# Wider weight rows, and another order of the output rows, in a decode block on one NeuronCore

## The chip, the cores and the metric

The kernel runs on one core of a Trainium2 chip. The metric is the device time of one launch in microseconds. The kernel before takes 121.06 us, the median of six runs (121.66, 121.75, 120.92, 120.96, 121.12 and 121.01 us).

## What is computed

A decode step for 8 sequences of one token each (B = 8, D = 512): a layer norm, and on its result two branches. Branch A is attention with 32 query heads over 8 key/value heads, on the last 1024 positions of a 4096-long cache (W = Sk // 4). Branch B is a gated feed-forward net with F = 1792. They meet in the last line.

```
xn = _layernorm(x)
q  = xn @ wq                                  # [512, 4096], 32 heads of 128
p  = softmax(q @ k[last 1024].T * 128**-0.5)  # 8 kv heads, 4 queries to each
s  = (p @ v[last 1024]) @ wo                  # [4096, 512]
g  = silu((gelu(xn @ w_gate) * (xn @ w_up)) @ w_down)
out = x + s * g                               # [8, 512]
```

All inputs are bf16. Keys and values of the window are 16 MB each, wq and wo 4 MB each, the three feed-forward weights 1.75 MB each (MB of 2^20 bytes here; the profile's page counts in 10^6).

## The kernel before

**Tiles and loads.** The attention is cut into 16 groups g = (b, i): one sequence b, and the half i of the kv heads (HN = 4 heads); the loop runs over i outside and b inside. A group needs one K tile and one V tile of 1 MB each: [128 partitions, 4096] bf16, so a partition holds 8 KB. All loads of weights, keys and values go into one ring of NSLOT = 20 such slots (`slot()`), and SyncE (SP) issues them in program order: wq in four pieces of 128 rows (L85, 8 KB to a partition) with the first K tile behind the first piece; then the second K tile, and in the loop V of group g and K of group g + 2 (L90). In the last group follow w_gate, w_up and w_down in two halves each (L100, L110: 7 KB to a partition), and in the round after it wo (L120, L125). The seven pieces of wo hold 8, 8, 8, 4, 2, 1 and 1 of its 32 steps, a step being one contraction of 128 rows; a partition takes four consecutive rows of wo per head group, so what lies together is 4 KB (2 and 1 KB in the last pieces). Between the third and the fourth piece four small loads put x into `x_res` (L499).

The framework gives the DMAs eight completion semaphores in turn, so each DMA of SP also waits until the eighth DMA before it has landed.

**A group.** TensorE transposes K (`turn_k`, L247, into PSUM; copied out by VectorE and ScalarE, L253), multiplies with the query (`score`, L263 and L273), ScalarE takes the exponential (L286), VectorE transposes it (L294), TensorE multiplies with V (`values`, L307), and `gather` (L323, L327, L336, L337) sums, divides and writes the head outputs into `oT_all`, laid out [d, half, kv head, query, b]. In round g the scores of group g stand before the values and the gather of group g - 1.

**Before the groups.** xhat (L210), [8, 512] padded to 32 rows, is transposed twice: in 128-column blocks for wq (L220), and with a stride of four for the feed-forward weights, whose partition p holds rows 4p to 4p + 3 (L223). The query projection is 32 matmuls (L375), eight for each piece of wq.

**The end.** After each half of the groups `regroup(i)` brings `oT_all` into the order of the rows of wo: 16 matmuls with columns of the identity (L350) and one copy into `og` (L359). Then `ffn_up` has 16 matmuls with w_gate and 16 with w_up (L418), the gelu (L430 to L442) and a VectorE transpose (L445); `ffn_down` has 28 matmuls (L461) and the silu (L473 to L480). The output projection is 64 matmuls (L537): for each of the 32 steps of wo, one for each half of the 512 columns. The two of a step sit on different columns of the array and run side by side; they are called a pair below. Two VectorE operations (L548, L549) and two small stores end the kernel. The schedule is written out by hand[...].

Of the kernel before, what the change touches and what calls it, by code (L numbers as in the profile page):

```python
# [11 lines left out]
BF16 = mybir.dt.bfloat16  # L12
FP32 = mybir.dt.float32
# [3 lines left out]
def kernel(  # L17
# [13 lines left out]
    nc = tc.nc  # L31

    B, Sq, D = A_x.shape
    Hkv, Sk, Dh = A_k_cache.shape[1], A_k_cache.shape[2], A_k_cache.shape[3]
    Hq = A_wq.shape[1] // Dh
    rep = Hq // Hkv
# [10 lines left out]

    NHALF = 2
    HN = Hkv // NHALF
    NSLOT = 20  # L50
    SLOT = NSC * Dh * HN
    NKR = W * HN // P
    QW = HN * rep
# [1 line left out]
    FR = F // P  # L55

    consts = ctx.enter_context(tc.tile_pool(name="consts", bufs=1))
    ring = ctx.enter_context(tc.tile_pool(name="ring", bufs=NSLOT))
    persist = ctx.enter_context(tc.tile_pool(name="persist", bufs=1))
    kT_pool = ctx.enter_context(tc.tile_pool(name="kT_pool", bufs=2))  # L60
# [13 lines left out]
    def slot():  # L74
        return ring.tile([P, SLOT], BF16, name="slot", align_bytes=512)

    x_flat = A_x.flatten_outer_dims()
    x_sb = persist.tile([B, D], BF16, name="x_sb")
    x_res = persist.tile([P, D // 2], BF16, name="x_res")
    nc.gpsimd.memset(x_res, 0.0)  # L80


    def load_wq(k):
        t = slot()
        nc.sync.dma_start(out=t, in_=A_wq[k * P : (k + 1) * P, :])  # L85
        return t

    def load_kv(cache, b, i):
        t = slot()
# [5 lines left out]
        )  # L95
        return t

    def load_up(w, k2):
        t = slot()
        nc.sync.dma_start(  # L100
            out=t[:, 0 : 2 * F],
            in_=w.rearrange("(p k) n -> p (k n)", k=NDC)[:, 2 * k2 * F : 2 * (k2 + 1) * F],
        )
        return t

    def load_down(h):
        t = slot()
        n = FR // 2 * D
        rows = B_w_down.rearrange("(p j) d -> p (j d)", j=FR)
        nc.sync.dma_start(out=t[:, 0:n], in_=rows[:, h * n : (h + 1) * n])  # L110
        return t

    wo_rows = A_wo.rearrange("(hh p j) d -> p hh (j d)", p=P, j=rep)

    def load_wo(h0, j0, j1):

        t = slot()
        n = (j1 - j0) // rep if j1 - j0 > rep else 1
        if n > 1:
            nc.sync.dma_start(  # L120
                out=t[:, 0 : n * rep * D].rearrange("p (h f) -> p h f", h=n),
                in_=wo_rows[:, h0 : h0 + n, :],
            )
        else:
            nc.sync.dma_start(  # L125
                out=t[:, 0 : (j1 - j0) * D],
                in_=wo_rows[:, h0, j0 * D : j1 * D],
            )
        return t

    groups = [(b, i) for i in range(NHALF) for b in range(B)]
# [1 line left out]
    k_t, v_t = {}, {}  # L133
    wq_t = [load_wq(0)]
    k_t[0] = load_kv(A_k_cache, *groups[0])
    wq_t += [load_wq(k) for k in range(1, NDC)]
    k_t[1] = load_kv(A_k_cache, *groups[1])


# [14 lines left out]
        base=0,  # L154
        pattern=[[-1, P]],
        channel_multiplier=1,
    )
    ident_f = consts.tile([P, P], FP32, name="ident_f")
    nc.vector.tensor_copy(out=ident_f, in_=ident)
# [55 lines left out]
        op0=ALU.subtract,  # L215
        op1=ALU.mult,
    )
    xT_ps = ps_t.tile([P, 2, NDC, 32], BF16, name="t_ps", tag="t")
    for k in range(NDC):
        nc.tensor.transpose(  # L220
            xT_ps[:, 0, k, :], xhat[:, k * P : (k + 1) * P], ident[0:32, 0:32]
        )
        nc.tensor.transpose(  # L223
            xT_ps[:, 1, k, :],
            xhat.rearrange("b (p k) -> b k p", k=NDC)[:, k, :],
            ident[0:32, 0:32],
        )
    xT = persist.tile([P, 2, NDC, 32], BF16, name="xT")
    nc.vector.tensor_copy(out=xT, in_=xT_ps)

    q2_all = persist.tile([P, NHALF, B, 2, 2, HN, rep], BF16, name="q2_all")
    nc.gpsimd.memset(q2_all, 0.0)
    oT_all = persist.tile([P, NHALF, HN, rep, B], BF16, name="oT_all")
    og = persist.tile([P, Hkv * rep + 1, 32], BF16, name="og")
    nc.vector.memset(og, 0.0)

    kT_t, p_t, pT_t, ss_t, o_t = {}, {}, {}, {}, {}
# [80 lines left out]
    def gather(g):  # L320
        b, i = groups[g]
        a_ps = ps_a.tile([P, 2, QW], FP32, name="a_ps", tag="a")
        nc.tensor.matmul(  # L323
            a_ps[:, 0, :], ones_f, ss_t[g], start=True, stop=True, skip_group_check=True
        )
        for r in range(2):
            nc.tensor.matmul(  # L327
                a_ps[:, 1, :],
                o_t[g][:, r * Dh : (r + 1) * Dh],
                selr[:, r, :],  # L330
                start=(r == 0),
                stop=(r == 1),
                skip_group_check=True,
            )
        rs = small.tile([P, QW], FP32, name="rs")
        nc.vector.reciprocal(out=rs, in_=a_ps[:, 0, :])  # L336
        nc.vector.tensor_tensor(  # L337
            out=oT_all[:, i, :, :, b],
            in0=a_ps[:, 1, :].rearrange("p (n j) -> p n j", n=HN),
            in1=rs.rearrange("p (n j) -> p n j", n=HN),  # L340
            op=ALU.mult,
        )

    def regroup(i):

        rg = ps_a.tile([P, rep, HN, B], FP32, name="rg_ps", tag="a")
        sel = ident.rearrange("p (e j) -> p j e", j=rep)
        for j in range(rep):
            for c in range(rep):
                nc.tensor.matmul(  # L350
                    rg[32 * c : 32 * c + 32, j, :, :],
                    sel[:, j, :],
                    oT_all[:, i, :, c, :],
                    start=True,
                    stop=True,
                    skip_group_check=True,
                    tile_position=(0, 32 * c),
                )
        nc.vector.tensor_copy(  # L359
            out=og[:, i * HN * rep : (i + 1) * HN * rep, 0:B].rearrange(  # L360
                "p (h j) b -> p h j b", j=rep
            ),
            in_=rg.rearrange("p j h b -> p h j b"),
        )


# [4 lines left out]
    for k in range(NDC):  # L371
        for i in range(NHALF):
            for j in range(HN):
                n0 = (HN * i + j) * 512
                nc.tensor.matmul(  # L375
                    q_ps[i][32 * j : 32 * j + 32, :],
                    xT[:, 0, k, :],
                    wq_t[k][:, n0 : n0 + 512],
                    start=(k == 0),
                    stop=(k == NDC - 1),  # L380
                    tile_position=(0, 32 * j),
                    skip_group_check=True,
                )
# [28 lines left out]
    def ffn_up():  # L412
        z_ps = ps_big.tile([P, 512], FP32, name="big")
        u_ps = ps_big.tile([P, 512], FP32, name="big")
        for ps, ws in ((z_ps, wg_t), (u_ps, wu_t)):
            for k in range(NDC):
                for j in range(4):
                    nc.tensor.matmul(  # L418
                        ps[32 * j : 32 * j + 32, 0:FT],
                        xT[:, 1, k, :],  # L420
                        ws[k // 2][:, (k % 2) * F + j * FT : (k % 2) * F + (j + 1) * FT],
                        start=(k == 0),
                        stop=(k == NDC - 1),
                        tile_position=(0, 32 * j),
# [30 lines left out]
    def ffn_down(hT):  # L455
        f_ps = ps_big.tile([P, 512], FP32, name="big")
        for j in range(FR):
            for t in range(2):
                w = wd_t[j // (FR // 2)]
                c0 = (j % (FR // 2)) * D + t * 256  # L460
                nc.tensor.matmul(  # L461
                    f_ps[64 * t : 64 * t + 32, 0:256],
                    hT[:, j, :],
                    w[:, c0 : c0 + 256],
                    start=(j == 0),
                    stop=(j == FR - 1),
                    tile_position=(0, 64 * t),
# [17 lines left out]
    for g in range(NGR + 1):  # L485
# [2 lines left out]
            if g + 2 < NGR:  # L488
                k_t[g + 2] = load_kv(A_k_cache, *groups[g + 2])
        if g == NGR - 1:  # L490
            wg_t = [load_up(B_w_gate, 0), load_up(B_w_gate, 1)]
            wu_t = [load_up(B_w_up, 0), load_up(B_w_up, 1)]
            wd_t = [load_down(0), load_down(1)]
        if g == NGR:

            parts = [(0, 0, 8), (2, 0, 8), (4, 0, 8), (6, 0, 4), (7, 0, 2), (7, 2, 3), (7, 3, 4)]
            wo_t = [load_wo(*q) for q in parts[:3]]
            for t, b0, b1 in ((0, 0, 1), (0, 1, 3), (0, 3, 8), (1, 0, 8)):
                nc.sync.dma_start(  # L499
                    out=x_res[64 * t + b0 : 64 * t + b1, :],  # L500
                    in_=x_flat[b0:b1, t * 256 : (t + 1) * 256],
                )
            wo_t += [load_wo(*q) for q in parts[3:]]
        if g < NGR:
            score(g)
            soft(g)
# [10 lines left out]
            turn_k(g + 1, 3)  # L517
        if g:
            gather(g - 1)
            if groups[g - 1][0] == B - 1:  # L520
                regroup(groups[g - 1][1])

    hT = ffn_up()
    ffn_down(hT)
# [2 lines left out]


    s_ps = ps_big.tile([P, 512], FP32, name="big")
    rows = []  # L530
    for q, (h0, j0, j1) in enumerate(parts):
        for j in range(j0, j1):
            rows.append((q, j - j0, h0 + j // rep, j % rep))
    for n, (q, at, hh, j) in enumerate(rows):
        for t in range(2):
            c0 = at * D + t * 256
            nc.tensor.matmul(  # L537
                s_ps[64 * t : 64 * t + 64, 0:256],
                og[:, hh * rep + j : hh * rep + j + 2, :].rearrange("p m b -> p (m b)"),
                wo_t[q][:, c0 : c0 + 256],  # L540
                start=(n == 0),
                stop=(n == len(rows) - 1),
                tile_position=(0, 64 * t),
                skip_group_check=True,
            )
    tmp = ffn_sb.tile([P, 256], BF16, name="tmp")
    out_sb = ffn_sb.tile([P, 256], BF16, name="out_sb")
    nc.vector.tensor_tensor(out=tmp, in0=s_ps[:, 0:256], in1=g_sb, op=ALU.mult)  # L548
# [34 lines left out]
```

## Time and profile before

| | |
|---|---|
| median of six runs | 121.06 us |
| the profiled execution, its time | 121.16 us |
| its span, first to last instruction | 119.5 us |
| its mean granted TensorE clock | 0.871 |
| TensorE matmul busy | 90.9 us (76%) |
| VectorE busy | 65.0 us (54%) |
| ScalarE busy | 40.5 us (34%) |
| DMA packets of SP's queue, share of 16 engines | 95.2% |
| read from HBM | 47.46 MB, 397 GB/s over the span |

The page gives busy times, forty slices of the span, the DMA queues, the chain of work that ended last, and groups of instructions by line. The time lies 1.66 us over the span, which begins with the first instruction and ends with the last. A packet is one descriptor's transfer on one of the 16 DMA engines; a DMA over 128 partitions gives eight packets to each engine, and has landed when the last of the 16 has reported.

### The profile page before, as it was taken

What the parts mean: (1) busy time and instruction counts of PE and PEld (TensorE: products, weight loads), DVE (VectorE), ACT (ScalarE), POOL (GpSimd) and SP (SyncE); (2) the same over time, 40 slices, a digit from 0 to 9 for tenths busy, and PEclk for the clock granted to TensorE, in tenths of its full rate; (3) what the DMA queues carried; (4) which work ended last, traced back from release to release, by engine and by line L of the source; (5) the groups of instructions that cost most, each with busy time, mean ns of one, the idle gap of its engine ahead of it and who ended that gap; (6) DMA issues with size and microseconds to landing.
All of it is one profiled execution on the core that took longest, in us unless ns stands there. A gap on an engine that the chain in (4) does not pass through costs nothing.

```text
span 119.5 us, 2371 instructions
## 1 busy us (share of the span) xinstructions
PE 90.9 (76%) x964; PEld 64.9 (54%) x964; DVE 65.0 (54%) x149; ACT 40.5 (34%) x78; POOL 3.8 (3%) x9
## 2 busy tenths in 40 slices
PE   0039549786999999999988997977979973394690
PEld 0038215563867777786775784665747640063570
DVE  5444244645567866866694874855847424704002
ACT  4003023692433562464353362362433303002000
POOL 6600000000000000000000000000000000000000
PEclk9999965568599999999999999999999755559689
DMA  3999999999999999999999999999999999999940
GB/s 77 416 420 439 428 417 428 436 422 414 431 436 428 417 417 436 422 422 422 431 425 417 428 433 428 417 425 431 433 414 427 420 427 423 422 414 422 408 164 3
DMA packets 7530, 47.62 MB, mean 399 GB/s; under 512 B 824, under 2 KB 1120, under 8 KB 2912
## 3 DMA queue, kind: packets, MB, share of 16 engines
q1 hardware_dynamic: 7488, 47.46, 95.2%
q8 instruction: 7, 0.11, 0.3%
q14 instruction: 3, 0.02, 0.0%
q10 hardware_dynamic: 32, 0.01, 0.0%
HBM read 47.46 MB, written 0.01 MB: 397 GB/s over the span
## 4 chain that ended last, share of the span: by engine, by line
DMA 58%; PE 23%; DVE 9%; ACT 4%; SPq 2%; issue 1%; DVEq 0%
DMA slot<-in_A_k_cache_dram 16%; DMA slot<-in_B_w_gate_dram 16%; DMA slot<-in_A_wo_dram 15%; PE t_ps L247 11%; DMA slot<-in_A_wq_dram 10%; DVE kT L253 5%; PE o_ps L307 4%; PE sc_ps L273 3%; PE big L537 2%; ACT q_all L404 2%; DVE q_all L404 2%; SPq L85 1%; ACT L286 1%; PE t_ps L396 1%; DVE q_sb L388 1%
## 5 line engine op out<-in xcount | busy, mean ns | idle before, releaser
L253 DVE COPY kT<-t_ps 128x1024 bf16<-128x1024 bf16 x48 | 31.8, 688 | 22.2 <-PE t_ps L247 20.2
L247 PE MATMUL t_ps<-ident_f,slot 128*128 128x128 f32 x256 | 38.9, 303 | 4.2 <-DMA slot<-in_A_k_cache_dram 4.2
L247 PEld LDWEIGHTS t_ps<-ident_f,slot 128*128 128x128 f32 x256 | 31.4, 154 | 14.0 <-issue 7.9
L253 ACT COPY kT<-t_ps 128x1024 bf16<-128x1024 bf16 x16 | 16.2, 1012 | 12.6 <-PE t_ps L247 12.3
L286 ACT ACTIVATE p<-sc_ps 128x512 bf16<-128x512 f32 x16 | 9.6, 597 | 29.9 <-PE sc_ps L273 29.9
L273 PE MATMUL sc_ps<-kT,q_all 128*32 128x512 bf16 x128 | 10.5, 397 | 3.4 <-DVE kT L253 1.7
L294 DVE STREAM_TRANSPOSE pT<-p 128x512 bf16<-128x512 bf16 x16 | 11.2, 702 | 2.7 <-ACT p L286 2.7
L307 PE MATMUL o_ps<-slot,pT 128*32 128x256 bf16 x256 | 10.6, 288 | 0.0
L327 PE MATMUL a_ps<-selr,o_sb 128*128 128x16 f32 x64 | 10.0, 270 | 0.3 <-ACT o_sb L317 0.3
L327 PEld LDWEIGHTS a_ps<-selr,o_sb 128*128 128x128 f32 x64 | 8.8, 200 | 0.5 <-ACT o_sb L317 0.4
L537 PE MATMUL big<-slot,og 128*64 128x256 bf16 x64 | 5.8, 333 | 2.8 <-DMA slot<-in_A_wo_dram 2.7
L273 PEld LDWEIGHTS <-q_all 128*32 128x32 bf16 x128 | 3.1, 94 | 7.7 <-issue 3.2
L307 PEld LDWEIGHTS <-pT 128*32 128x32 bf16 x256 | 5.6, 98 | 2.9 <-issue 2.5
L537 PEld LDWEIGHTS <-og 128*64 128x64 bf16 x64 | 4.8, 134 | 4.1 <-issue 2.6
L317 ACT COPY o_sb<-o_ps 128x256 f32<-128x256 f32 x16 | 6.0, 378 | 1.6 <-PE o_ps L307 1.6
L263 PE MATMUL sc_ps<-far,hot 4*128 4x512 bf16 x16 | 6.4, 397 | 0.0
L323 PEld LDWEIGHTS a_ps<-ss,ones_f 128*128 128x128 f32 x32 | 5.1, 202 | 0.6 <-issue 0.6
L220 PE MATMUL t_ps<-ident,xhat 32*128 32x32 bf16 x4 | 0.4, 188 | 6.5 <-DVE xhat L210 6.5
L323 PE MATMUL a_ps<-ss,ones_f 128*128 128x16 f32 x32 | 5.1, 236 | 0.0
L418 PE MATMUL big<-slot,xT 128*32 128x448 bf16 x32 | 3.5, 567 | 2.1 <-DMA slot<-in_B_w_up_dram 2.1
L336 DVE RECIPROCAL rs<-a_ps 128x16 f32<-128x16 f32 x16 | 4.0, 248 | 1.9 <-PE a_ps L327 1.8
L461 PE MATMUL big<-slot,hT 128*32 128x256 bf16 x28 | 3.4, 417 | 1.8 <-DVE hT L445 1.7
(63 smaller groups left out, 51.5 us busy)
## 6 DMA issues: line engine op xcount, KB each, us to landing
slot<-in_A_k_cache_dram SPq DMA_DIRECT2D x16, 1024.0 KB, 19.6
slot<-in_A_v_cache_dram SPq DMA_DIRECT2D x16, 1024.0 KB, 19.6
slot<-in_A_wq_dram SPq DMA_DIRECT2D x4, 1024.0 KB, 10.6
slot<-in_A_wo_dram SPq DMA_DIRECT2D x3, 1024.0 KB, 18.1
slot<-in_B_w_gate_dram SPq DMA_DIRECT2D x2, 896.0 KB, 19.5
slot<-in_B_w_up_dram SPq DMA_DIRECT2D x2, 896.0 KB
slot<-in_B_w_down_dram SPq DMA_DIRECT2D x2, 896.0 KB, 18.1
slot<-in_A_wo_dram SPq DMA_DIRECT2D x1, 512.0 KB, 8.6
```

The source lines that it names most:

```text
L247: nc.tensor.transpose(kp[:, c * P : (c + 1) * P], kw[:, rp * P : (rp + 1) * P], ident_f)
L253: copy(out=kT_t[g][:, t * 8 * P : (t + 1) * 8 * P], in_=kp.bitcast(BF16))
L263: nc.tensor.matmul(sc, hot.rearrange("n r q -> n (r q)"), far, start=True, stop=False, skip_group_check=True,)
L273: nc.tensor.matmul(sc[32 * t : 32 * t + 32, :], q2_all[:, i, b, e, :, :, :].rearrange("w r n j -> w (r n j)"), kT[:, :, 32 * t : 32 * t + ...
L286: nc.scalar.activation(out=p, in_=sc_t[g], func=ACT.Exp, scale=inv_sqrt_dh, accum_out=acc)
L294: nc.vector.transpose(out=pT, in_=p)
L307: nc.tensor.matmul(o_ps[32 * u : 32 * u + 32, :], pT_t[g][:, m * 32 : (m + 1) * 32], v_t[g][:, m * 256 : (m + 1) * 256], start=(m < 4), st ...
L317: nc.scalar.copy(out=o_sb, in_=o_ps)
L323: nc.tensor.matmul(a_ps[:, 0, :], ones_f, ss_t[g], start=True, stop=True, skip_group_check=True)
L327: nc.tensor.matmul(a_ps[:, 1, :], o_t[g][:, r * Dh : (r + 1) * Dh], selr[:, r, :], start=(r == 0), stop=(r == 1), skip_group_check=True,)
L404: copy(out=q2_all[64 * rr : 64 * rr + 64, i, :, e, rr, :, :].rearrange("p b n j -> p j n b"), in_=qT_ps[64 * rr : 64 * rr + 64, :, e, :, 0:B],
L537: nc.tensor.matmul(s_ps[64 * t : 64 * t + 64, 0:256], og[:, hh * rep + j : hh * rep + j + 2, :].rearrange("p m b -> p (m b)"), wo_t[q][:, ...
```

## The change

- wq lies in SBUF as the feed-forward weights do, rows 4p to 4p + 3 on partition p, and comes in two DMAs of 2 MB with 16 KB to a partition. The first transposition of xhat (L220) goes, and all weights use the other.
- w_gate, w_up and w_down come in one DMA each, 14 KB to a partition. These, wq and the first piece of wo use a pool of three wide slots of 2 MB; the ring has 14 slots instead of 20 and holds keys, values and the rest of wo. The third wide slot takes w_gate and then the first piece of wo.
- wo lies with rows 32p to 32p + 31 on partition p. Its pieces hold 16, 8, 4, 2, 1 and 1 steps, so the largest packet is 16 KB. Two loads of `x_res` take the place of four.
- `oT_all` becomes [d, b, head]. `regroup` runs once, between the matmuls of w_gate and w_up: one VectorE transpose of [128, 256] in 32 x 32 blocks, one matmul with a permutation matrix `perm`, one copy into `og`. GpSimd makes `perm` from the identity at the start.

```diff
-    NSLOT = 20
+    NSLOT = 14
+    NWIDE = 3
+    wide = ctx.enter_context(tc.tile_pool(name="wide", bufs=NWIDE))
+    wq_rows = A_wq.rearrange("(p k) n -> p (k n)", k=NDC)
+    def load_wide(rows, c0, c1):
+        t = wide_slot()
+        nc.sync.dma_start(out=t[:, 0 : c1 - c0], in_=rows[:, c0:c1])
...
-    wo_rows = A_wo.rearrange("(hh p j) d -> p hh (j d)", p=P, j=rep)
+    wo_rows = A_wo.rearrange("(p j) d -> p (j d)", j=NOR)
...
+    nc.gpsimd.tensor_copy(
+        out=perm.rearrange("p (h q) -> p h q", q=P // 32),
+        in_=ident.rearrange("p (q h) -> p h q", q=P // 32),
+    )
...
-        rg = ps_a.tile([P, rep, HN, B], FP32, name="rg_ps", tag="a")
-        sel = ident.rearrange("p (e j) -> p j e", j=rep)
-        for j in range(rep):
-            for c in range(rep):
-                nc.tensor.matmul(
-                    rg[32 * c : 32 * c + 32, j, :, :],
-                    sel[:, j, :],
-                    oT_all[:, i, :, c, :],
...
+        zt = ffn_sb.tile([P, B * Hq], BF16, name="zt")
+        nc.vector.transpose(out=zt, in_=oT_all.rearrange("p b h -> p (b h)"))
+        rg = ps_a.tile([P, B, 32], FP32, name="rg_ps", tag="a")
+        nc.tensor.matmul(
+            rg.rearrange("p b j -> p (b j)"),
+            perm,
+            zt,
...
         nc.vector.tensor_copy(
+            out=og[:, 0:NOR, 0:B], in_=rg.rearrange("p b j -> p j b")
         )
...
         for ps, ws in ((z_ps, wg_t), (u_ps, wu_t)):
+            if ps is u_ps:
+                regroup()
...
-            parts = [(0, 0, 8), (2, 0, 8), (4, 0, 8), (6, 0, 4), (7, 0, 2), (7, 2, 3), (7, 3, 4)]
-            wo_t = [load_wo(*q) for q in parts[:3]]
-            for t, b0, b1 in ((0, 0, 1), (0, 1, 3), (0, 3, 8), (1, 0, 8)):
+            parts = [(0, 16), (16, 24), (24, 28), (28, 30), (30, 31), (31, 32)]
+            wo_t = [load_wo(*q) for q in parts[:2]]
+            for t in range(2):
...
-            if groups[g - 1][0] == B - 1:
-                regroup(groups[g - 1][1])
```

## The prediction, made before the changed kernel was run

> **What bounds the kernel now.** I read the slices first, then the queue's share, the waits, the stretches of the end and its timeline.
>
> ```profile
> PE   0039549786999999999988997977979973394690
> DMA  3999999999999999999999999999999999999940
> q1 hardware_dynamic: 7488, 47.46, 95.2%
> ```
>
> The DMA engines are full from the second slice to the last but two; TensorE is full only in the middle, where it catches up. In the waits SyncE waits almost only for landings of earlier DMAs (25.0 us for K, 20.5 us for V), eight DMAs back, some 20 us of work queued ahead. So the bytes set the time, and two things can be gained: the cost of a byte, and what stands between the last byte and the end. The end, from the stretches (columns: busy of PE, PEld, DVE, ACT, POOL, granted clock, DMA share, GB/s):
>
> ```profile
> 112.00:113.00 1.00, 1.00 (x10) 0.72 (x7) 0.00 (x0) 0.00 (x0) 0.00 (x0) 0.50 1.02 412
> 113.00:114.00 1.00, 0.54 (x7) 0.53 (x7) 0.23 (x1) 0.00 (x0) 0.00 (x0) 0.50 0.88 343
> 114.00:115.00 1.00, 1.00 (x17) 1.00 (x15) 0.00 (x0) 0.00 (x0) 0.00 (x0) 0.71 0.69 243
> 115.00:116.00 1.00, 1.00 (x16) 0.63 (x12) 0.00 (x0) 0.00 (x0) 0.00 (x0) 1.00 0.27 91
> ```
>
> Some DMA engines run dry 2 us before others: each DMA's first and last engine report 1.7 to 2.0 us apart (0.5 us before 25 us). The slowest stays full to 115.7, and it counts. TensorE is full too in the last 2 us, and its clock rises from 0.5 to 1.0 there. The output projection in the timeline (start, length):
>
> ```profile
> 108.56 1.06 PE L537 MATMUL big<-slot,og 128*64 128x256 bf16 x16 [0.77 <-DMA slot<-in_A_wo_dram]
> 111.11 1.90 PE L537 MATMUL big<-slot,og 128*64 128x256 bf16 x16 [1.49 <-DMA slot<-in_A_wo_dram]
> 113.47 2.89 PE L537 MATMUL big<-slot,og 128*64 128x256 bf16 x32 [0.46 <-DMA slot<-in_A_wo_dram]
> ```
>
> The last two matmuls start at 116.06, 0.04 us after the last piece landed (116.02; the four before it 113.43, 114.70, 115.34, 115.68), and end at 116.36. With the last 3.1 us (L548, L549, store) that is the span of 119.5. In this execution the transfer won by a hair. A pair starts every 213 ns at clock 0.5 and every 109 ns at 1.0. The clock record changes at 107.76, 111.17 and 114.58: steps of 3.41 us.
>
> [...] 8192 B took 309 ns, 7168 B 272, 4096 B 159, 1024 B 46; a line through them is 9 ns and 0.0366 ns a byte. [...] a full clock after a window some 85% busy (111.17 to 114.58), none after one at 62%. [...] If the rise comes late, the 16 pairs after 113.47 take 16 x 213 = 3.41 us and end at 116.88 instead of 116.17, 0.71 us later; the two longest runs of before (121.66, 121.75) stand 0.68 us over the mean of the other four (121.02).
>
> **The change, part by part.**
>
> Packets, for each of 16 engines. wq: 32 to 16, 16 x 9 = 0.144 us. Feed-forward weights: 48 to 24, 0.216. wo's first 16 steps: 32 to 8, 0.216; the next 8: 16 to 8, 0.072. wo's last pieces keep their sizes. Fewer DMAs: wq 2, feed-forward 3, wo 1, x_res 2, each with a completion packet of 9 ns, 0.07. Sum 0.72 us, on the slowest engine too. Bounds: no load of before has a 16 KB packet, but instruction fetches are 16384 B: the shortest took 880 ns while it shared an engine, less one 7168 B packet 272 is 608, what the line gives (609). So I take 0.72, with 0 (a long row at a 32 KB pitch is no cheaper) and 1.0 (waits between packets fall too) as ends.
>
> Landings that follow: wo's first 16 steps 111.07 - 0.63 = 110.44, the next 8 112.73, the last 116.02 - 0.72 = 115.30.
>
> The start. K of group 0 lands behind 3 MB instead of 2, 2.4 us later (about 10.7), and its transposes (3.67 us) end before wq is in (15.5). Then 16 query matmuls are left instead of 8: four steps of four at up to 0.43 us instead of two, +0.8 us for the first scores. Cover: loads run 8 DMAs ahead, and TensorE makes 4.15 us a group against 4.9 of transfer until it meets the loads at about 54 to 60 us; the delay is gone there. Uncovered it would cost 0.8. GpSimd's copy for `perm` (128x128; a select of that size took 0.29) delays hot and far, needed only at 19.5, and they were ready by 4.1; four transposes of xhat fewer save 0.1, hidden.
>
> The ring. A load now waits for the tile 14 loads back rather than 20. V of group 7 needs V of group 0 free (about 31.6 us), and waits for its eighth predecessor until about 35 anyway. Nothing.
>
> The middle regroup goes (16 matmuls, 0.32 us in slack). The last one: VectorE transpose, half of 702 ns = 0.35; one matmul of 256 columns, 0.4; copy of 128x256, twice 0.29. TensorE meets it after w_gate's matmuls at about 98.7, and w_up lands at 101.3: hidden by 2 us.
>
> w_gate: all 16 matmuls wait for one landing (97.37 - 0.24 of packets = 97.13) and end at 98.65, as before (98.68). Behind this stands the new wait: SyncE issues wo's first piece only when they are done, since it takes their slot; queued behind it are all of wo and x_res. At 98.7 the ring still holds w_up's rest and w_down, whose fastest engine ends at about 103.7; issue to first packet is about 1.7 us, so 3 us are spare. Late beyond that it costs one for one.
>
> w_up: 16 matmuls after 101.31, 1.5 us instead of 0.75 after 101.64: gelu's end, hT, +0.4. w_down: 28 matmuls after 105.65 rather than 14, 3.0 us at half clock: end 108.7 instead of 107.78. The next piece of wo comes at 110.44, so hidden by 1.7; the silu (2.4 us) ends at about 111.2.
>
> The output projection loses its head start. 32 pairs are left from 110.44, where before 16 were left from 113.47. With the clock rising at 114.58 again: 19.2 pairs by then, 12.8 x 109 = 1.39, last pair done at 115.97 against 116.17: gain 0.2 instead of 0.72. A rise before about 113.3 makes the landing the bound: gain 0.72 against this profile. Against a late-clock run of before the gain is larger, about 0.7 to 1. Over both the middle is 0.55: 121.16 - 0.55 = 120.6 from the profiled execution; from the runs' median, which is 0.1 lower, 120.5. I take 120.5.
>
> **The rivals.** D, the forecast (40%): both bounds near each other, 120.5. A (28%): the landing alone is the bound, because the clock rises early: 121.06 - 0.72 = 120.3 or less. For it: the DMA view, and the run of w_down's matmuls, 3 us without a gap, that can raise the clock for the window after it. Against: at half clock TensorE has 6.8 us of work after 110.44, and 4.9 us until the last landing. B (18%): the transfer gains nothing, 121.1: what 8 KB gained over 4 KB (26.5 against 25.8 GB/s an engine) need not come again at 16 KB, or the slowest engine becomes another, since one fetch packet of 0.9 us that falls on it outweighs the 0.72. C, slower (14%): TensorE takes the end. If the clock rises at time r, the last pair ends at r + (32 - (r - 110.44)/0.213) x 0.109; that passes before's 116.17 from r = 115.0 on and 116.8 from r = 116.3 on; all at half clock it is 117.3, 1.1 us over before. 121.06 + 0.6 = 121.7 for its middle. For it: the clock was 0.5 from 111.17 to 114.58. Against: 32 pairs without a gap fill a window soon.
>
> **How the numbers follow.** The measurement tells about 0.5%, 0.6 us, from no change, so faster means below 120.45. D lies on that line and splits: 22 of its 40 faster, 18 the same. A is faster. B is the same, but a fifth of it slower. C is slower, save 3 of 14 that are the same. Faster 0.50, the same 0.35, slower 0.15. Range: 119.9 (1.0 us of packets, an early clock and 0.15 of the runs' scatter) to 121.4 (B with scatter and the near half of C).
>
> **What would show it.** Queue share and bytes as before, about 1280 packets fewer (1152 of data); 16 KB packets at about 609 ns; the last landing 0.7 us earlier; the output matmuls in one run of 32 or more from about 110.4, and their last pair at most 0.3 us after the last landing if the clock rose early, up to 1 us if late. The wait of SyncE for TensorE's w_gate matmuls near 98.7, with no gap in DMA near 104. Wrong if a DMA slice before the end falls under full, if 16 KB packets take over 640 ns, or if the first landings of K lag beyond 60 us.

## The result, and the profile after

The kernel after takes 120.84 us (median of 34 runs) and the kernel before, run beside it, 121.13 us (69 runs): a ratio of 0.9966, 95% interval 0.9954 to 0.9977. A second set of runs on another chip gave 120.80 us (13 runs) beside 121.11 (66), 0.9955 [0.9933, 0.9978]. So the change gains about 0.3 to 0.5 us. That is inside the predicted range, but on the other side of the 0.5% line from the likeliest case: 120.5 was 0.3 us too good.

The times of both kernels fall into two groups. Of before, 40 runs lie around 121.03 us and 29 around 121.69; of after, 26 around 120.80 and 8 around 121.23. The gain is 0.23 us between the medians of the two lower groups; the rest of what an average shows comes from the upper group, which in after is smaller and nearer (121.07 to 121.34).

The slices of after and its queue, from the page:

```profile
PE   0014946786999999999998797976979853546680
PEclk9999999555899999999999999999999955556999
DMA  4999999999999999999999999999999999999940
q1 hardware_dynamic: 6240, 47.46, 95.0%
```

The DMA row is as full as before, with 1248 packets fewer (7488 to 6240) for the same bytes, and the queue's share hardly moved (95.2% to 95.0%): what the packets saved is small against what they carry.

The stretches of the end (columns: busy of PE, PEld, DVE, ACT, POOL, granted clock, DMA share, GB/s) and the output projection in the timeline (start, length):

```profile
112.00:113.00 1.00, 0.56 (x12) 0.39 (x7) 0.00 (x0) 0.00 (x0) 0.00 (x0) 1.00 0.96 387
113.00:114.00 1.00, 0.86 (x16) 0.86 (x16) 0.23 (x1) 0.00 (x0) 0.00 (x0) 1.00 0.91 341
114.00:115.00 1.00, 0.78 (x12) 0.45 (x9) 0.00 (x0) 0.00 (x0) 0.00 (x0) 1.00 0.49 177
115.00:116.00 1.00, 0.97 (x10) 0.43 (x7) 0.00 (x0) 0.00 (x0) 0.00 (x0) 1.00 0.05 17
```

```profile
105.86 3.17 PE L453 MATMUL big<-wide_slot,hT 128*32 128x256 bf16 x28 [2.63 <-DMA wide_slot<-in_B_w_down_dram]
110.62 1.94 PE L523 MATMUL big<-wide_slot,og 128*64 128x256 bf16 x32 [1.59 <-DMA wide_slot<-in_A_wo_dram]
113.14 1.06 PE L523 MATMUL big<-slot,og 128*64 128x256 bf16 x16 [0.58 <-DMA slot<-in_A_wo_dram]
114.43 1.55 PE L523 MATMUL big<-slot,og 128*64 128x256 bf16 x16 [0.22 <-DMA slot<-in_A_wo_dram]
```

The granted clock is 1.0 from 109.19 us on. Its record changes at 20.44, 30.68, 95.54 and 109.19 us, whole multiples of 3.41 us apart as in before, but 1.43 us off before's steps; a step is called a window below, and where the steps lie the raster. In the window ahead of the rise, from 105.78 to 109.19, w_down's 28 matmuls kept TensorE 93% busy. So the output projection runs at full clock, and ahead of each of its three stretches TensorE waits for a DMA. The last piece lands at 115.64 (before 116.02), the last pair starts 0.04 us later (its two matmuls 3 ns apart), and the span is 119.1 us (before 119.5). In this execution the transfer sets the end, and it ends 0.38 us earlier. The span itself is 0.32 us shorter (119.45 to 119.13): 0.06 us are lost again behind the output's landing, for a reason that the experiments with one DMA more bring up.

The regroup in its new place, between w_gate's and w_up's matmuls (TensorE's timeline):

```profile
97.30 1.69 PE L411 MATMUL big<-wide_slot,xT 128*32 128x448 bf16 x16 [1.36 <-DMA wide_slot<-in_B_w_gate_dram]
98.92 0.40 PE L346 MATMUL rg_ps<-zt,perm 128*128 128x256 bf16 x1
101.54 1.69 PE L411 MATMUL big<-wide_slot,xT 128*32 128x448 bf16 x16 [2.23 <-DMA wide_slot<-in_B_w_up_dram]
```

After the permutation matmul TensorE idles 2.23 us until w_up has landed. And SyncE's waits (total, times, longest) show the new wait for TensorE that the wide slot brought:

```profile
SPq L93 <- DMA wide_slot<-in_B_w_gate_dram: 16.1, 1, 16.1
SPq L93 <- PE rg_ps L346: 2.0, 1, 2.0
```

SyncE issues wo's first piece at 99.03. No DMA slice near 104 falls under full, so this wait costs nothing.

### The profile page after: what moved, and what is told of

The parts are those of the page before. It is cut to its first block, busy times and chain, and to the rows that moved or that the text cites. A ratio compares the mean times of both kernels' runs of the same rounds, so it can differ in the third digit from the quotient of the medians.

```text
span 119.1 us, 2281 instructions
## 1 busy us (share of the span) xinstructions
PE 86.6 (73%) x929; PEld 62.1 (52%) x929; DVE 64.1 (54%) x149; ACT 40.5 (34%) x78; POOL 4.3 (4%) x10
## 2 busy tenths in 40 slices
DMA packets 6281, 47.61 MB, mean 400 GB/s; under 512 B 728, under 2 KB 1024, under 8 KB 1280
## 3 DMA queue, kind: packets, MB, share of 16 engines
q1 hardware_dynamic: 6240, 47.46, 95.0%
## 4 chain that ended last, share of the span: by engine, by line
DMA 58%; PE 21%; DVE 11%; ACT 4%; SPq 2%; issue 1%; DVEq 0%
DMA wide_slot<-in_B_w_gate_dram 18%; DMA slot<-in_A_v_cache_dram 16%; DMA slot<-in_A_wo_dram 12%; DMA wide_slot<-in_A_wq_dram 11%; PE t_ps L244 10%; DVE kT L250 8%; PE sc_ps L270 4%; PE o_ps L304 3%; ACT q_all L395 2%; DVE q_all L395 2%; PE big L411 1%; PE big L523 1%; ACT L283 1%; PE big L366 1%; DVE q_sb L379 1%
## 5 line engine op out<-in xcount | busy, mean ns | idle before, releaser
L244 PE MATMUL t_ps<-ident_f,slot 128*128 128x128 f32 x256 | 38.4, 300 | 8.0 <-DMA slot<-in_A_k_cache_dram 8.0
L270 PE MATMUL sc_ps<-kT,q_all 128*32 128x512 bf16 x128 | 10.7, 405 | 3.9 <-ACT q_all L395 1.9
L304 PE MATMUL o_ps<-slot,pT 128*32 128x256 bf16 x256 | 9.9, 275 | 0.0
L411 PE MATMUL big<-wide_slot,xT 128*32 128x448 bf16 x32 | 3.4, 573 | 3.6 <-DMA wide_slot<-in_B_w_up_dram 2.2
L523 PEld LDWEIGHTS <-og 128*64 128x64 bf16 x64 | 3.5, 109 | 3.7 <-DMA wide_slot<-in_A_wo_dram 2.1
L220 PE MATMUL t_ps<-ident,xhat 32*128 32x32 bf16 x4 | 0.3, 193 | 6.7 <-DVE xhat L210 6.7
L453 PE MATMUL big<-wide_slot,hT 128*32 128x256 bf16 x28 | 3.2, 418 | 2.6 <-DMA wide_slot<-in_B_w_down_dram 2.6
L453 PEld LDWEIGHTS <-hT 128*32 128x32 bf16 x28 | 2.3, 144 | 3.8 <-DVE hT L438 3.4
```

The lines of the kernel that those rows point to most:

```text
L244: nc.tensor.transpose(kp[:, c * P : (c + 1) * P], kw[:, rp * P : (rp + 1) * P], ident_f)
L270: nc.tensor.matmul(sc[32 * t : 32 * t + 32, :], q2_all[:, i, b, e, :, :, :].rearrange("w r n j -> w (r n j)"), kT[:, :, 32 * t : 32 * t + ...
L304: nc.tensor.matmul(o_ps[32 * u : 32 * u + 32, :], pT_t[g][:, m * 32 : (m + 1) * 32], v_t[g][:, m * 256 : (m + 1) * 256], start=(m < 4), st ...
L453: nc.tensor.matmul(f_ps[64 * t : 64 * t + 32, 0:256], hT[:, j, :], wd_t[:, c0 : c0 + 256], start=(j == 0), stop=(j == FR - 1), tile_positi ...
```

## The experiments

**Theories.** T1: landing and clock. The packets save less than their records say, about 0.4 us at the last landing, and the two groups of times are early and late rises of TensorE's clock. T2: the packets save the predicted 0.72 us, and something else (the wait for w_gate's matmuls, the regroup, the lost head start, or instruction fetches that fall on the slowest DMA engine) takes half of it back.

### Only the loads of before, only the loads of after

Both kernels leave out all arithmetic; the output is x plus a slice of wo. All loads keep order, size and slots.

```diff
-    for t in range(4):
-        turn_k(0, t)
...
-    hT = ffn_up()
-    ffn_down(hT)
...
+    nc.vector.tensor_tensor(out=out_sb, in0=wo_t[-1][:, 0:256], in1=x_b, op=ALU.add)
```

> All loads of the kernel before in their order and from the same ring of slots, and none of the arithmetic: the output is x plus a slice of wo. Both theories of the missing 0.3 us expect the same of this run alone: it is the base for the next one. With hardly any instructions there are few instruction fetches, so the engines of one DMA should report within 0.6 us of each other to the end (1.9 us in the kernel before), and the last landing should come about 1.2 us earlier than 116.02 us after the start of the span, near 114.8.

> All loads of the changed kernel, none of the arithmetic, so without the wait for the w_gate matmuls; output as in e1. Theory 1, neighbouring packets overlap, so that a packet costs about 5 ns of an engine's time and not the 9 ns of its record: the last landing 0.40 us before that of e1, the time shorter by 0.3 to 0.5 us. Theory 2, a packet costs the full 9 ns and the rest was lost to instruction fetches that fell on the slowest engine: 0.65 to 0.72 us before e1.

The loads of before alone take 119.10 us (ratio 0.9814 [0.978, 0.9847]), those of after 118.49 (0.9762 [0.9729, 0.9795]); the last landings are 114.58 and 113.92. Their queues, narrow first:

```profile
q1 hardware_dynamic: 7488, 47.46, 96.6%
```

```profile
q1 hardware_dynamic: 6240, 47.46, 96.7%
```

The difference is 0.66 us at the landing and 0.61 in time. That is what T2 forecast (0.65 to 0.72 at the landing) and more than T1's 0.40, so by the total alone T1 missed. The intervals between landings show what the total is made of. 2 MB took 2 x 2.454 = 4.908 us with 8 KB packets and 4.855 with 16 KB: 0.053 over 8 packets saved, 6.6 ns each. Two pieces of 0.875 MB with 7 KB packets took 2 x 2.147 = 4.294, one with 14 KB packets 4.263: 3.9 ns each. wo with 4 KB packets took 2.493 us a MB: (2 x 2.493 - 4.855) / 24 = 5.5 ns each. So a packet less is worth 4 to 7 ns, not the 9 of the records: neighbouring packets overlap. (These are differences of 0.03 to 0.13 us, and the completion packets of the DMAs saved, 4 B and 9 ns each on record, are in them.) The DMA share of 1.02 in a stretch of before had been the hint. On the mean of the 16 engines the loads of after gain 0.36 us after the first 2 MB, as 5 ns say; another 0.14 lies ahead of that point, and 0.16 in a narrower spread between the first and the last engine (0.27 us against 0.44). These last two do not show in the full kernels: there the mean engine gains 0.40 after the first 2 MB, and the spread is 1.7 to 1.9 us in both. So T1 has the price of a packet, and T2 is right in one point: something that the loads alone do not have takes back what the spread gained. What it is comes with the last experiment.

### A warm clock in both kernels

Idle matmuls of 512 columns (their result is not used) keep TensorE busy where it would wait: 23 in before (the text of its forecast says 25), 22 in after.

```diff
+    def warm(n):
+        w_ps = ps_sc.tile([P, 512], FP32, name="sc_ps")
+        q_flat = q2_all.rearrange("p i b e r n j -> p (i b e r n j)")
+        for _ in range(n):
+            nc.tensor.matmul(
+                w_ps, ident, q_flat[:, 0:512], start=True, stop=True, skip_group_check=True
+            )
...
                 regroup()
+                warm(6)
...
+    warm(8)
     ffn_down(hT)
+    warm(8)
```

The calls shown are those in after; in before there are three each ahead of the two halves of w_up, six behind `ffn_up`, three behind `ffn_down`, and five and three in the output projection.

> The kernel before, with 25 matmuls of 512 columns that nobody reads put into the waits of TensorE from w_up on, so that its clock is full in the output projection. If the two groups of times of the kernel before (around 121.03 and around 121.69 us) come from the clock, the later group goes: the median falls to 120.95 to 121.05 and no run lies over 121.4. If they come from the transfer, about 4 of 10 runs stay at 121.7.

> The changed kernel with 22 such matmuls in the waits after the regroup, after w_up and after w_down. If the clock makes the late runs (8 of 34 near 121.2), they go and the median is 120.7 to 120.8; the distance to e3 is then the difference of the last landings alone, 0.25 to 0.4 us by theory 1 and 0.6 to 0.7 us by the forecast's sum. If the transfer makes them, the share of late runs stays.

Before with a warm clock: spans of 119.2 to 119.8 us in 14 runs, where the kernel before on the same chip has 14 of 32 runs at 119.7 to 120.6, 12 of them at 119.9 or more. The group of late ends is gone from the spans. The forecast for the times missed: the median of 121.25 (0.9998 [0.9973, 1.0023]) is no better, and six runs lie over 121.4. Eight of the 14 runs take 1.8 to 2.8 us more than their span, where before beside it takes 1.7 to 1.8; why is open. The one lead is in the profiled execution (122.11 us, 2.8 over its span): alone among the traces it has an eighth 16384 B instruction fetch, 1.8 us after the end of the span (121.10), which took 1.31 us. After with a warm clock: 120.69 us (19 runs), 0.9947 [0.993, 0.9964], spans of 119.0 to 119.3 without a late one. Its output projection is that of after, though TensorE had 22 matmuls more:

```profile
110.64 1.94 PE L534 MATMUL big<-wide_slot,og 128*64 128x256 bf16 x32 [1.02 <-DMA wide_slot<-in_A_wo_dram]
113.10 1.06 PE L534 MATMUL big<-slot,og 128*64 128x256 bf16 x16 [0.52 <-DMA slot<-in_A_wo_dram]
114.40 1.62 PE L534 MATMUL big<-slot,og 128*64 128x256 bf16 x16 [0.24 <-DMA slot<-in_A_wo_dram]
```

For before, then, the two groups are the clock, as T1 has it: same chip, same loads, and the late ends go. For after the same is likely but less directly shown: after was not run without the idle matmuls on this chip, and on the chip of the second set it had no late run among 13 either. With the clock out of the way the change is worth 119.4 - 119.0 = 0.4 us of median span (spans are on record to 0.1 us): the landing.

### The regroup twice

```diff
             if ps is u_ps:
                 regroup()
+                regroup()
```

> The changed kernel with the regroup (VectorE transpose, permutation matmul, copy) done twice in the same place. Forecast: hidden before w_up lands, so 120.84 us within 0.1. If it stands on the path that sets the end, about 1.2 us more (0.45 + 0.40 + 0.42 by the profile of the changed kernel).

121.01 us (22 runs), 0.9966 [0.9946, 0.9986]. That is 0.17 over the forecast, on a chip on which before too was slower (121.52 us, 43 runs), and far from 1.2 us; the shortest run, 120.57, is as short as any of after. The second permutation matmul starts at 100.16, still ahead of w_up's at 101.51. The regroup is hidden. The profiled execution of this kernel was its longest (121.98 us), and shows what the rival C of the prediction looks like:

```profile
105.75 3.17 PE L454 MATMUL big<-wide_slot,hT 128*32 128x256 bf16 x28 [2.56 <-DMA wide_slot<-in_B_w_down_dram]
110.60 3.62 PE L524 MATMUL big<-wide_slot,og 128*64 128x256 bf16 x32 [1.68 <-DMA wide_slot<-in_A_wo_dram]
114.02 3.15 PE L524 MATMUL big<-slot,og 128*64 128x256 bf16 x32
```

```profile
115.00:116.00 1.00, 1.00 (x14) 0.82 (x12) 0.00 (x0) 0.00 (x0) 0.00 (x0) 0.50 0.05 15
116.00:117.00 1.00, 1.00 (x16) 0.80 (x12) 0.00 (x0) 0.00 (x0) 0.00 (x0) 0.73 0.00 0
```

The same 28 matmuls of w_down, 0.11 us earlier, do not bring the clock up here: the raster lies 0.5 us later, its window from 106.30 to 109.71 is 77% busy and the next 74%, and only the one from 113.12 on is full. (A third execution, after on the chip of the second set, lies between: its window from 106.03 to 109.44 was 86% busy, and the clock rose.) The output projection runs without a gap, at half clock until 116.54, and ends at 117.2, 1.7 us after the last landing (115.52); the span is 120.3.

### The head start given back

wo's first 16 steps as two pieces of 8 in the ring, so that TensorE can begin at 108 and SyncE does not wait for w_gate's matmuls; the second kernel has the idle matmuls too.

```diff
-            parts = [(0, 16), (16, 24), (24, 28), (28, 30), (30, 31), (31, 32)]
-            wo_t = [load_wo(*q) for q in parts[:2]]
+            parts = [(0, 8), (8, 16), (16, 24), (24, 28), (28, 30), (30, 31), (31, 32)]
+            wo_t = [load_wo(*q) for q in parts[:3]]
...
```

> The changed kernel with the first piece of wo cut into two of 8 steps, through the ring of narrow slots as in the kernel before, so that wo's first load waits for no matmul. Clock theory: TensorE gets its head start of 8 pairs back, so the late group of runs shrinks from 0.43 us above the early one to 0.2 us or less, no span lies over 119.5 us, and the early runs stay at 120.8 (one more DMA and 8 more packets to an engine cost 0.04 us). If the order of the loads and the wait for w_gate had cost something of their own, the early runs would fall by 0.2 us or more.

> The changed kernel with both: the idle matmuls that keep the clock full (14 in the feed-forward part, 8 between the pieces of wo) and wo's first piece in two. If the transfer is the only bound left once the clock is full, the same as with the idle matmuls alone: 120.65 to 120.75, all spans within 119.0 to 119.3. If the head start is worth something beyond the clock, 0.1 us or more below that.

Both missed: 121.41 us (14 runs), 1.0003 [0.9982, 1.0023], and 121.35 (14 runs), 0.9998 [0.9977, 1.0019]. In the first, whose profiled execution was its longest (121.81 us), the last landing came at 116.07. In the second the last landing (115.50) and the last pair are earlier than in after, so there the loss lies behind the matmuls. In both one of the eight completion semaphores had changed: with one DMA more the output's store got another, and among SyncE's last waits, which stand in a fixed order, that one comes third instead of last. My theory was now that this order costs the 0.5 us. Three kernels tested it, with after beside them on the same chip.

### One DMA more, and the split with the DMA count of after

The first only cuts a load of `x_res` in two; the second splits wo but joins two of its last pieces; the third is the second with idle matmuls.

```diff
-            for t in range(2):
+            for t, b0, b1 in ((0, 0, 4), (0, 4, 8), (1, 0, 8)):
...
```

```diff
-            parts = [(0, 16), (16, 24), (24, 28), (28, 30), (30, 31), (31, 32)]
+            parts = [(0, 8), (8, 16), (16, 24), (24, 28), (28, 31), (31, 32)]
...
```

> The kernel after with x_res loaded in three DMAs instead of two (4, 4 and 8 rows), nothing else. One DMA more ahead of the output's store moves the store to another of the eight completion semaphores, as in the split kernel. If the semaphore's place among SyncE's last waits costs the 0.5 us (my theory), every execution becomes 0.5 to 0.6 us longer: median 121.3 to 121.4, shortest about 121.15, and from the end of the last matmul to the end of the span 3.6 to 3.7 us instead of 3.12. If the split of wo itself cost the time (more DMAs in flight, the slot of another ring), this kernel stays at 120.7 to 120.9 with 3.1 us there.

> The split of wo's first 16 steps into two of 8 (TensorE gets its head start back, and no wait on w_gate's matmuls), with the last pieces 4, 3 and 1 steps instead of 4, 2, 1 and 1, so that there are as many DMAs as in the kernel after and the store keeps its semaphore. Clock theory: the shorter group of times stays at 120.7 to 120.85, the later group is gone or at most 0.2 above it; span never over 119.6. If the split itself costs 0.5 us: 121.3 to 121.4 again.

> The split with the same count of DMAs, and idle matmuls as in the warmed kernel after (6 after the regroup, 8 after w_up's, 4 at each of two places in the output projection). Landing alone is the bound then: 120.6 to 120.75, spans 118.9 to 119.2 in all executions. If the split costs by itself: 121.2 to 121.4.

> The kernel after, unchanged, on the chip of the three kernels beside it, so that they are compared with it directly. Expected: 120.7 to 120.9 for most executions, and about one in four 0.4 us above.

Measured: 121.23 us (22 runs; 0.9997 [0.998, 1.0014]), 121.03 (22; 0.9971 [0.9955, 0.9986]), 121.10 (22; 0.998 [0.9965, 0.9995]), and after 120.80. The semaphore theory fell: in the kernel with one DMA more, SyncE was through with all its waits 0.20 us after the store had landed (0.04 in after), so the order costs at most 0.16 us, and in the split kernel the store keeps its semaphore and still 0.2 us are lost. None of the 22 spans of the split is over 119.5 us, as forecast, while the kernel with one DMA more, which has no head start, reaches 120.1; but after itself stayed at 119.4 or less in its 13 runs here, so what the head start is worth is not shown.

What is common to all of them stands in SyncE's records at the end. Each has one gap of 0.44 to 0.48 us between two instructions, and 0.63 us after it an instruction fetch of 8192 B on queue q14 (us from the span's start; the gap ends where SyncE's next instruction starts):

```
kernel                    gap from  to       gap   fetch    store lands  end
after                     118.64    119.11   0.48  119.75   118.24       119.13
split, same count         118.22    118.66   0.45  119.29   118.37       119.53
one DMA more              118.85    119.32   0.48  119.95   118.37       119.65
split                     118.67    119.13   0.45  119.75   118.65       120.10
warm, split               118.12    118.57   0.45  119.20   118.10       119.55
warm, split, same count   118.01    118.46   0.44  119.08   118.16       119.31
```

In before the corresponding fetch is at 110.16, while SyncE waits for a landing anyway (until 111.09). The gap sits at a fixed place in the program: in all nine traces of after and its variants it stands ahead of the 80th of SyncE's recorded instructions, while their number runs from 80 to 87. In after the 80th is SyncE's very last, and the gap costs 0.10 us (the other engines' last instructions start at 119.02). Each instruction added to SyncE's stream moves it forward, into the last waits. From the store's landing to the end it is 0.83 us in before, 0.89 in after (so this change moved the gap there, and pays the 0.06 us), 1.16 in the split with the same count, 1.28 with one DMA more and 1.45 in the split: 0.27, 0.39 and 0.56 more than in after (the two warm kernels, 1.15 and 1.44, repeat their cold counterparts). The times say the same: 121.03 - 120.80 = 0.23; 121.18 (the 15 runs with spans up to 119.6) - 120.80 = 0.38; 121.41 - 120.80 = 0.6, this one across two chips. That SyncE waits for its next instructions in the gap is my reading of the records, from the fetch behind it and its fixed place; no run moved it alone.

### The loads of after with instruction fetches

What makes the spread of 1.7 us between the DMA engines in the full kernels, when the loads alone have 0.3? In the traces it jumps from 0.5 to 1.7 us with the first 16384 B instruction fetch (at 25.65 us in before, 27.38 in after). Six more follow in either kernel and leave further engines behind, but the spread stays between 1.5 and 2.0. The loads of after with 612 idle matmuls test it; the arithmetic is left out as before.

```diff
+        for _ in range(36):
+            nc.tensor.matmul(
+                i_ps, idle[:, 0:32], idle[:, 32:64], start=True, stop=True, skip_group_check=True
+            )
...
```

> The loads of e2 and 612 matmuls of 32 columns on zeros, that nothing waits for: about 1225 instructions of TensorE, as many as in the changed kernel, and no other arithmetic. If the instruction fetches make the engines of one DMA report 1.1 us further apart (0.3 us in e2), the fetch packets come back, the spread grows to about 1.4 us or more and the last landing comes 1.0 to 1.3 us later than in e2 (113.92): a time near 119.6. If the spread comes from the arithmetic's own traffic, it stays at 0.3 us and the time at 118.5.

119.87 us (6 runs; 0.9874 [0.984, 0.9909]) against 118.49 without the matmuls (on another chip). Four fetches came, from 6.89 to 27.83 us. Below them the first K tile's load without and with the matmuls (both issued at 1.2 us; the last figure is from issue to landing):

```profile
q8 instruction: 4, 0.07, 0.2%
slot<-in_A_k_cache_dram SPq DMA_DIRECT2D x1, 1024.0 KB, 9.2
slot<-in_A_k_cache_dram SPq DMA_DIRECT2D x1, 1024.0 KB, 10.6
```

They took 0.9 us each, the spread went from 0.3 to 1.6 us, and the last landing from 113.92 to 115.35, while the first engine to finish moved by 0.09 (113.65 to 113.74). Nearly all of this is there after the first fetch: the K tile landed at 11.78 instead of 10.37, 1.41 us later, against 1.43 at the end. The other three fetches fell on other engines; at the end four of the 16 report 1.4 to 1.6 us after the first, and the rest within 0.25. The 1225 TensorE instructions of this kernel came with four fetches, the 929 matmuls and 929 weight loads of after with seven. So a fetch left one DMA engine 1.1 to 1.4 us behind the others for good: each engine has the same eight packets of a load (8 x 309 ns = 2.47 us, against 2.454 between the landings of 1 MB in the loads alone), and the load has landed when the last engine reports, as the K tile's 1.41 us show. That TensorE's instructions are fetched while the loads run costs these loads 1.4 us at the last landing; how many fetches there are hardly matters.

## Why the prediction was right or wrong, point by point

**What bounds the kernel: right.** The DMA engines are full to the end in both (95.2% and 95.0% of the span), and the last landing decides in most executions.

**The packets: the step that failed.** The mechanism was right, with 1248 packets fewer (about 1280 predicted) and 16 KB packets at 611 ns (609 predicted). The price was not: 9 ns is the intercept of the packet's own duration, and 4 to 7 ns is what the queue gained for each. With these, wq is 16 x 6.6 = 0.11, the feed-forward weights 24 x 3.9 = 0.09, wo's first 16 steps 24 x 5.5 = 0.13 and the next 8 steps 8 x (2.493 - 2.454) us / 8 = 0.04 in all: 0.37 us instead of 0.72. The last landing moved by 0.38. That the two agree so well is in part luck: the profiled execution of before was 0.13 us longer than the middle of its group, and the last landings in profiled executions with the loads of after scatter from 115.52 to 115.78 us (after, its second set, the warm clock, the regroup twice, one DMA more), with those of before 115.88 and 116.02. Their means are about 0.3 us apart; less the 0.06 us at SyncE's end, that is near the 0.23 us between the lower groups. The other landings: wo's first piece at 110.58 instead of the predicted 110.44, the next at 113.10 instead of 112.73. The records do show a fixed cost per packet, 9 ns, but a record of one packet does not measure what it costs among its neighbours, here 4 to 7 ns.

**The start: hidden, as predicted; its size hangs on the clock.** K of group 0 landed at 10.63 (10.7 predicted): its 16 reports came from 10.21 to 10.63, and SyncE issued the eighth DMA after it at 10.64. The query matmuls of after, and of after with idle matmuls (which come only behind 98 us):

```profile
15.53 1.05 PE L366 MATMUL big<-wide_slot,xT 128*32 128x512 bf16 x16 [0.50 <-DMA wide_slot<-in_A_wq_dram]
14.88 2.77 PE L366 MATMUL big<-wide_slot,xT 128*32 128x512 bf16 x32
```

In after the clock was full to 20.44, the 16 that were left took 1.05 us together, and the first scores came at 20.0 us against 20.4 before. But in that execution of before the clock had fallen to 0.5 at 15.60. In the second line the clock rose only at 16.67; until then a step of four took 0.42 us, the price that the prediction used, and the first scores came at 21.12, while before with idle matmuls, whose clock fell at 18.50, had them at 19.87. So the delay exists when the clock is low, and that the pair above shows none is luck of the clock. It was hidden in either case: in the late one the last landing came at 115.68.

**Ring, regroup, the new wait: right.** The doubled regroup cost nothing; TensorE had 2.2 us to spare there. SyncE issued wo's first piece at 99.03 (98.7 predicted) without a gap in DMA. w_down ended at 109.03 (108.7 predicted), 1.59 us ahead of the next piece. One reading was off without harm: from issue to first packet before shows 1.0 to 1.3 us (0.80 to 1.83; 113.49 to 114.76), not 1.7.

**The output projection: right in mechanism.** At full clock the landing is the bound (rival A's way, at half its price), and at half clock TensorE is (rival C). By their times 26 of 34 runs went the first way, and on the chip of the second set all 13. With 0.38 in place of 0.72, A's 120.3 becomes 121.06 - 0.38 = 120.7, near the 120.80 of the lower group. The upper group stands 0.43 us higher. The prediction's formula for the last pair, started at 110.62, gives these times (121.07 to 121.34) for a clock that rises between 114.6 and 115.2 us, at or just after the 114.58 of the forecast's middle case; this is an estimate, since none of these eight runs was profiled. So the middle case is what the slower quarter of the runs did, and the number 120.5 joined a gain of 0.72 that no run had to a late clock that most did not have. The prediction's support from the runs of before was a little better than it said: the other four average 121.00, so the two longest stand 0.70 us over them, beside the 0.71 it had worked out.

**Rival B** said that nothing is gained, or that a fetch decides which engine is slowest. Half of it holds: fetches set the slowest engine in both kernels, by about the same amount (a spread of 1.67 us after the first one in either), so that the narrower spread of wide packets (0.16 us in the loads alone) is lost.

**Rival C, slower.** Its place and its size are shown by the twofold regroup's profiled execution, whose span of 120.3 is 1.2 us over after's: with its rise at 116.54, C's formula, started at 110.60, has the last pair done at 117.0, and the pair started at 116.89. No run of after itself was that late, and before has the same mechanism more often: 29 of 69 runs in the upper group against 8 of 34. The raster did not follow the work: the same 28 matmuls filled a window to 93% in one execution and to 77% in another whose raster lay 0.5 us later, and only the first got the full clock.

**The last 3.1 us of the span are not fixed.** The prediction took them as such. From the end of the last matmul they were 3.09 us in before and 3.15 in after; with some instructions more on SyncE they become 3.4 to 3.7.

## What to carry to other kernels

Price a packet by the interval between landings of whole loads, not by the intercept of packet records: here 1152 data packets fewer were worth about 0.37 us of 121. When DMA sets the time, look at the spread between the first and the last of the 16 engines, and for the instruction fetches that make it. Here the first fetch made nearly all of it (0.5 to 1.67 us), so a stream somewhat shorter would have gained little; a kernel with its arithmetic and no fetch while the loads run was not tried. Of the versions run, after with idle matmuls (120.69 us, no late group) has the lowest median, 0.11 us under after; they were on different chips, so that it beats after is not shown by a direct comparison. Its 19 runs lie between 120.62 and 120.96 us.

## What the runs showed of the hardware that was not expected

- A 16384 B instruction fetch (0.9 us) left one DMA engine 1.1 to 1.4 us behind the others for the rest of the kernel. In the loads with 612 idle matmuls the first fetch delayed the landings by 1.41 us, all four together by 1.43.
- SyncE showed a gap of 0.44 to 0.48 us ahead of an 8192 B fetch, in nine traces at the same place of its instruction stream (before the 80th on record). Near the end of the kernel it lengthened the run by 0.1 to 0.4 us, depending on SyncE's instruction count; the order of the last waits added up to 0.16 (0.20 less 0.04).
- Packet records overlapped: 9 ns of fixed time by their durations, 4 to 7 ns by the landings.
